# Strassen sums kept in PSUM, a second product in another order, and a planner that knows an exclusion

## The chip, the cores and the metric

The kernel runs on one core of a Trainium2 chip. The metric is device time in microseconds, the median of several runs; the profile shows one execution, with its span from the first instruction to the last. Five engines take part: TensorE (PE in the rows, its weight loads PEld), VectorE (DVE), ScalarE (ACT), GpSimd (POOL) and SyncE (SP), which issues most of the DMAs.

## The reference

Three parts follow each other, in float32, for a batch of 8 with 576 tokens and width 512:

1. Linear attention with 8 heads: `phi(x) = [exp(p), exp(-p)]` with `p = x @ w_phi - max|x @ w_phi|`, then `num / den` from `phi(k)^T v` and the sum of `phi(k)`.
2. A gated mixer: `(sigmoid(conv5(x)) * (x @ w_val)) @ w_out`, with a causal convolution of 5 taps per channel.
3. An FFT mixer and an MLP: `u = x + Re(fft2(x))`; `un` is the layer norm of `u`; the output is `u + relu(un @ w_ch1) @ w_ch2`, with 2048 hidden units.

This change lies in the third part, in the MLP and in the last FFT steps that are planned together with its start.

## The kernel before

Every product in float32 is made of float32r pieces: an operand is split into a rounded part `h` (made by ScalarE) and a rest `l = x - h` (a subtraction, on VectorE or GpSimd), and a product is three matmuls (`h*h`, `h*l`, `l*h`). A "split" below means both steps.

The MLP takes the tokens in 9 blocks of 512 (`NBK`) and the hidden units in 8 slices of 256 (`NJ`). Half of the weights is in SBUF at a time, so there are two passes over the blocks: the first with slices 0 to 3, blocks upwards, the second with slices 4 to 7, blocks downwards. A block of a pass is two units (`c` = 0, 1) of two slices each. The first pass computes the layer norm of each next block (`ln_stages`) and stores it; the second pass loads it again. Both passes make the seven split operands `un` of a block (`prep_un`) from tile `A`, of which there is one.

Both products of a unit use Winograd's form of Strassen's scheme: 7 products of 12 matmuls of 128x256 each instead of 8.

- `c1_units` makes the first product. Its seven products go to PSUM tiles `x` (two, used in turn by the units), `y` and `z`. ScalarE copies partial results to SBUF tiles `c11`, `c22` and `c12`; VectorE adds the later products to them; relu is on ScalarE; three subtractions of these SBUF tiles make the sums that Strassen's second product needs (noted after product 2), and each of the seven operands is split (`plain`, L813) into one of seven `h` slots.
- `c2_units` makes the second product from the `h` slots, in the order `SEQ2`, in PSUM tiles `cx`, `cy`, `cz`; `EVAC` says which tile a product goes to and to which of four SBUF accumulators `acc` VectorE then adds it.

The units are woven: the seven second products of one unit are noted between the seven first products of the next. Nothing is run in the order noted. `op` records an operation with what it reads and writes and with its cost for each engine that may do it: "v" VectorE, "a" ScalarE, "p" GpSimd, "m" TensorE, "d" DMA; "vp" leaves the choice between VectorE and GpSimd open. `place_ops` then plans: from the end backwards it gives each operation a due time, so that TensorE's work could run on without a gap; then, forwards, it takes again and again the operation that can start first on some engine, and among those ready on one engine the one due first. GpSimd gets an open operation only if it finishes it by the time VectorE would have, or by the due time. The engines' instruction order is the plan's order. `place_ops` runs twice: in `run_last` (the last two batches' FFT steps, the first block's layer norm and operands, the first weights) and in `run_mlp` (all the rest). Engine times (`free`) carry over from the first to the second.

The costs of the planner are a constant plus a slope per column, in microseconds (a matmul of the MLP has 0.109):

```
COST = {"v": (0.069, 1.042), "a": (0.09, 0.84), "p": (0.149, 2.1)}
```

Most of VectorE's and GpSimd's subtractions are recorded at the helpers' lines: L72 and L75 are the rests of a split on VectorE and on GpSimd, L648 any addition or subtraction, L651 a ScalarE copy or relu, L66 the rounded part of a split. L807 is the first product, L876 the second, L722 and L723 the means of the layer norm, L752 its reciprocal.

Of the kernel before, what the change touches and what calls it, by code (L numbers as in the profile page):

```python
# [23 lines left out]
TB = 512  # L24
# [5 lines left out]
def f32(ap):  # L30
    return ap.bitcast(F32)
# [3 lines left out]
def attention_moe_mixer_kernel(  # L35
# [540 lines left out]
    K = dict(hlo="vp", ht="vp", un="vp", ln="vp", w="vp", lat=0.2, lnat=6, bw=0.0028, dl=1.5, sq="a", su="a", ca=1, wl=1, win=0.0, marg=0.0, un0="vp", ln0="vp", w0="vp", t_lo="p", uf="vp")  # L576
# [7 lines left out]
    hs = []  # L584
# [47 lines left out]
    COST = {"v": (0.069, 1.042), "a": (0.09, 0.84), "p": (0.149, 2.1)}  # L632

    def op(e, cols, fn, reads, writes, dur=None, more=0.0):
        if dur is None:
            dur = {k: COST[k][0] + COST[k][1] * cols / 1000 for k in e}
        else:
            dur = {e: dur}
        ops.append((dur, fn, reads, writes, more))
# [4 lines left out]
    def o_lo(e, dst, src, hi, cols, r, w):  # L644
        op(e, cols, lambda e: (lo_dve if e == "v" else lo_pool)(dst, src, hi), r, w)

    def o_tt(e, o, x, y, alu, cols, r, w):
        op(e, cols, lambda e: (nc.vector if e == "v" else nc.gpsimd).tensor_tensor(out=o, in0=x, in1=y, op=alu), r, w)  # L648
# [143 lines left out]
    def c1_units(key, js):  # L792
# [5 lines left out]
        def product(i, n, first):  # L798
# [10 lines left out]
            op("m", 0, f, wk + [("un", i, 0), ("un", i, 1)] + ([] if first else [n]), [n, ("c1", key, i)], 12 * 0.109)  # L809
# [7 lines left out]
        def sub(o, p, r, e, rk, wk):  # L817
            o_tt(e, o, p, r, ALU.subtract, TB, rk, wk)

# [27 lines left out]
        s = sl[1] = h_free.pop(0)  # L847
        h, l = hs[s]
        o_act(h, x, ACTF.Relu, TB, [X], [("h", s, 0)])
        stt = nc.vector.scalar_tensor_tensor  # L850
        op("v", TB, lambda e: stt(out=l, in0=x, scalar=0.0, in1=f32(h), op0=ALU.max, op1=ALU.subtract), [X, ("h", s, 0)], [("h", s, 1)])
        plain(4, c11, "c11")
        plain(5, c22, "c22")
        plain(6, c12, "c12")
        op("v", TB, lambda e: stt(out=c22, in0=x, scalar=0.0, in1=c22, op0=ALU.max, op1=ALU.subtract), [X, "c22"], ["c22"])
        plain(3, c22, "c22")

    EVAC = {0: ("x", 0), 1: ("z", 0), 4: ("y", 3), 5: ("x", 1), 6: ("x", 3), 2: ("y", 1), 3: ("x", 2)}
    SEQ2 = (0, 1, 4, 5, 2, 6, 3)

    def c2_units(ps, t, c, key, js):
        for i in SEQ2:
# [15 lines left out]
            op("m", 0, f, wk + [("h", s, 0), ("h", s, 1)] + ([] if first else [ct]), [ct], 12 * 0.109)  # L878
# [23 lines left out]
    def note_W(b, ge, t, f, ps):  # L902
        gh, gl = ge
        for c in (0, 2, 1, 3):
            for a in range(2):
                k, p = next(ps)

                def prod(e, c=c, a=a, p=p):
                    for kk in range(4):
                        ws = slice(c * 128, (c + 1) * 128)  # L910
                        mm3(p[:, 0:NE], (wo[0][:, kk, ws], wo[1][:, kk, ws]), (gh[:, kk, a], gl[:, kk, a]), kk == 0, kk == 3)
                op("m", 0, prod, [], [k], 12 * 0.123)
                o_act(t[:, c, a, :], p[:, 0:NE], ACTF.Copy, NE, [k], [("x2", b, c, a)])
# [14 lines left out]
    def note_FD(b, f, y, ps):  # L928
# [4 lines left out]
        for j in range(3):  # L933
            n = 128 if j < 2 else 33
            sl = slice(128 * j, 128 * j + n)
            for a in range(2):
# [8 lines left out]
                op("m", 0, prod, fk + [("xr", 0), ("xr", 1)], [k], (7 - a) * 0.11)  # L945
# [18 lines left out]
    def note_SD(b, t, y, ps):  # L964
        yh, yl = y
        eo, u = tl["eo"], tl["u"]
        if b % 4 == 3:
# [3 lines left out]
               [("c256", e, i) for e in (b - 1, b) for i in range(5)], [k], 8 * 0.123)  # L971
# [6 lines left out]
        for i in range(2):  # L978
            ls = slice(128 * i, 128 * i + 128)
            for a in range(2):  # L980
# [6 lines left out]
                op("m", 0, prod, yk, [k], (8 - a) * 0.123)  # L987
# [82 lines left out]
    free = dict.fromkeys("mvapd", 0.0)  # L1070

    def place_ops():
# [3 lines left out]
        for i, (d, f, r, w, more) in enumerate(ops):  # L1076
# [19 lines left out]
        now = sum(o[0].get("m", 0) for o in ops)  # L1096
# [20 lines left out]
        end = [0.0] * n  # L1117
        for _ in range(n):
            best = None
            for e, q in ready.items():  # L1120
                cand = []
                for i in q:
                    d = ops[i][0]
                    if e == "p" and "v" in d:
                        t = max(free["p"], at[i])
# [14 lines left out]
            free[e] = t0 + ops[i][0][e]  # L1140
            start[i], end[i] = t0, free[e] + ops[i][4]
# [228 lines left out]
```

## Time and profile before

| | before |
|---|---|
| median of 3 runs | 1427.9 us (1426.38 to 1427.92) |
| profiled execution, span | 1426.1 us |
| TensorE busy, matmuls | 1346.5 us (94%) |
| VectorE busy | 1254.0 us (88%) |
| ScalarE busy | 814.0 us (57%) |
| GpSimd busy | 706.9 us (50%) |
| mean granted TensorE clock | 0.987 |

For the profiled execution the record has its span alone, and no total time of its own; the nearest run is 0.3 us above the span, the median 1.8 us. The attention takes about the first 320 us, the mixer and the FFT run to about 640, the MLP from there to the end. A VectorE record overlaps the next by about 0.08 us, so what an operation costs in a row of others is read from the distance of their starts.

### The profile page before, as it was taken

To read this page: it belongs to the slowest core of one execution; us is meant where nothing else is said; L and a number is where in the kernel's file an instruction comes from. 1 tells how busy PE (TensorE), PEld (TensorE's weight loads), DVE (VectorE), ACT (ScalarE), POOL (GpSimd) and SP (SyncE) were. 2 spreads that over 40 slices of the span, in tenths; PEclk is the share of its full clock that TensorE was granted. 3 is DMA by queue.
4 is the path that set the end of the run, shared out by engine and by line. 5 is a ranking of instruction groups with operands and counts; after the bars stand their busy time and mean duration, and the time that the engine had idled before them with its cause. 6 is when DMAs were issued, how large, how long until landed. Compare 5 with 4: busy or idle time off the path is not lost.

```text
span 1426.1 us, 35034 instructions
## 1 busy us (share of the span) xinstructions
PE 1346.5 (94%) x14672; PEld 1296.2 (91%) x14672; DVE 1254.0 (88%) x1938; ACT 814.0 (57%) x1513; POOL 706.9 (50%) x526
## 2 busy tenths in 40 slices
PE   8999989988999999967899899999999999999998
PEld 7888878877999999967799899999999999999998
DVE  6999999886999999798999999999899888778876
ACT  6888878763555545555455555555465455444442
POOL 3977888613576776464565455555335111111111
PEclk9999999998999999988999999999999999999999
DMA  7478867531344432335422232222433222122211
GB/s 257 149 259 301 275 240 254 207 148 52 104 141 141 141 139 103 120 129 181 134 93 93 90 119 92 94 82 89 141 109 104 82 81 84 60 90 90 89 42 48
DMA packets 89851, 186.98 MB, mean 131 GB/s; under 512 B 10455, under 2 KB 37335, under 8 KB 87518
## 3 DMA queue, kind: packets, MB, share of 16 engines
q1 hardware_dynamic: 88488, 181.33, 37.3%
q10 hardware_dynamic: 1206, 3.41, 0.6%
q8 instruction: 115, 1.88, 0.5%
q14 instruction: 42, 0.34, 0.1%
HBM read 121.79 MB, written 62.93 MB: 130 GB/s over the span
## 4 chain that ended last, share of the span: by engine, by line
PE 48%; DVE 34%; issue 6%; ACT 4%; POOL 4%; DMA 3%; SPq 0%; DVEq 0%; POOLq 0%; ACTq 0%
PE cx L876 9%; PE x L807 9%; PE cy L876 5%; PE y L807 4%; PE kv L244 4%; DVE acc L425 4%; PE pj L205 3%; DVE A L648 3%; DVE c L648 3%; PE nm L283 3%; PE z L807 3%; DVE acc L648 2%; PE cz L876 2%; DVE y L215 2%; DVE s L752 2%
## 5 line engine op out<-in xcount | busy, mean ns | idle before, releaser
L876 PE MATMUL cx<-h,w 128*128 128x256 f32 x1152 | 176.4, 286 | 4.8 <-ACT h L66 2.5
L876 PEld LDWEIGHTS cx<-h,w 128*128 128x128 f32 x1152 | 158.4, 194 | 6.8 <-ACT h L66 3.1
L66 ACT ACTIVATE h<-c 128x512 fp32r<-128x512 f32 x180 | 111.6, 627 | 38.9 <-DVE c L648 22.4
L648 POOL TENSOR_TENSOR c<-c,c 128x512 f32<-128x512 f32 x35 | 49.8, 1422 | 165.0 <-ACT h L651 125.4
L648 DVE TENSOR_TENSOR acc<-cx,acc 128x512 f32<-128x512 f32 x144 | 97.9, 680 | 33.0 <-PE cx L876 32.3
L651 ACT ACTIVATE c<-c 128x512 f32<-128x512 f32 x108 | 67.9, 630 | 100.4 <-DVE c L648 99.1
L807 PE MATMUL x<-un,w 128*128 128x256 f32 x864 | 117.0, 285 | 7.6 <-DVE eo L648 6.9
L75 POOL TENSOR_TENSOR h<-c,h 128x512 fp32r<-128x512 f32 x33 | 48.3, 1466 | 149.2 <-ACT h L66 148.9
L876 PE MATMUL cy<-h,w 128*128 128x256 f32 x864 | 117.3, 284 | 4.6 <-DVE h L72 1.9
L807 PEld LDWEIGHTS x<-un,w 128*128 128x128 f32 x864 | 109.9, 193 | 8.2 <-issue 7.1
L425 DVE SCALAR_TENSOR_TENSOR acc<-xf,cw,acc 128x576 f32<-128x576 f32 x128 | 104.9, 819 | 12.1 <-ACT acc L423 11.2
L876 PEld LDWEIGHTS cy<-h,w 128*128 128x128 f32 x864 | 108.9, 191 | 7.0 <-DVE h L72 2.5
L72 DVE TENSOR_TENSOR h<-c,h 128x512 fp32r<-128x512 f32 x111 | 103.7, 935 | 1.2 <-ACT h L66 0.5
L212 DVE TENSOR_REDUCE m<-pj 128x8 f32<-128x1024 f32 (+1 forms) x80 | 88.5, 1107 | 9.7 <-PE pj L205 9.7
L244 PE MATMUL kv<-vraw,ke 128*64 128x66 f32 x2560 | 95.6, 228 | 0.5 <-DVE kvT L257 0.2
L205 PE MATMUL pj<-wp,kqraw 64*128 64x128 f32 x1152 | 89.2, 293 | 6.2 <-DMA kqraw<-in_k_dram 4.4
L244 PEld LDWEIGHTS kv<-vraw,ke 128*64 128x64 f32 x2560 | 83.4, 139 | 11.5 <-ACT ke L224 1.0
L205 PEld LDWEIGHTS pj<-wp,kqraw 64*128 64x128 f32 x1152 | 73.5, 193 | 20.0 <-issue 20.0
L283 PE MATMUL nm<-kvT,qe 128*64 128x65 f32 x2304 | 84.3, 225 | 7.3 <-issue 4.1
L215 DVE TENSOR_TENSOR y<-pj,m 128x1024 f32<-128x1024 f32 (+1 forms) x80 | 88.6, 1107 | 0.4
L75 POOL TENSOR_TENSOR ge<-gs,ge 128x580 fp32r<-128x580 f32 x32 | 46.8, 1461 | 78.7 <-ACT ge L66 78.7
L283 PEld LDWEIGHTS nm<-kvT,qe 128*64 128x64 f32 x2304 | 76.5, 140 | 9.6 <-issue 7.7
(249 smaller groups left out, 4218.3 us busy)
## 6 DMA issues: line engine op xcount, KB each, us to landing
raw<-in_w_ch_dram SPq DMA_DIRECT2D x16, 1024.0 KB, 6.0
wr<-w_scr SPq DMA_DIRECT2D x32, 448.0 KB, 3.6
vraw<-in_v_dram SPq DMA_DIRECT2D x16, 660.0 KB, 9.3
x_scr<-xT SPq DMA_DIRECT2D x32, 288.0 KB, 4.0
xf<-x_scr SPq DMA_DIRECT2D x8, 1152.0 KB, 5.7
out_dram<-acc SPq DMA_DIRECT2D x36, 256.0 KB, 2.2
kqraw<-in_k_dram SPq DMA_DIRECT2D x15, 576.0 KB, 5.5
kqraw<-in_q_dram SPq DMA_DIRECT2D x15, 576.0 KB, 7.4
```

Source lines behind the costliest of these rows:

```text
L66: nc.scalar.activation(out=dst, in_=src, func=ACTF.Copy)
L72: nc.vector.tensor_tensor(out=dst, in0=src, in1=f32(hi), op=ALU.subtract)
L75: nc.gpsimd.tensor_tensor(out=dst, in0=src, in1=f32(hi), op=ALU.subtract)
L205: mm(p[:, h, o:o + F], t[r, w, 128 * c:128 * c + 128], wp[r, :], start=True, stop=True)
L212: nc.vector.tensor_reduce(out=m, in_=pv, axis=AX.X, op=ALU.max, apply_absolute_value=True)
L215: nc.vector.tensor_tensor(out=y, in0=pv, in1=m.unsqueeze(3).to_broadcast([128, 2, 2 * n, F]), op=ALU.subtract)
L244: mm(t[p, w, :], e[:, a, h, j, p], tv[:, h, slot, :], start=slot % 5 == 0 and w == 0, stop=slot % 5 == 4 and w == 3, skip_group_check=True)
L283: mm(t[p, 2 * j + h, 0:65], e[:, a, h, j, p], kt[:, 2 * h + a, b, :], start=(a == 0), stop=(a == 1))
L425: nc.vector.scalar_tensor_tensor(out=acc, in0=shifted(t), scalar=cw[:, m, t:t + 1], in1=acc, op0=ALU.mult, op1=ALU.add)
L648: op(e, cols, lambda e: (nc.vector if e == "v" else nc.gpsimd).tensor_tensor(out=o, in0=x, in1=y, op=alu), r, w)
L807: mm(p[:, n], l, v[:, kt], start=first and n + kt + m == 0, stop=kt == 1 and m == 2, skip_group_check=True)
L876: mm(p[:, o], v, r[:, n], start=first and o + n + m == 0, stop=n + m == 3, skip_group_check=True)
```

## The change

Four things are changed at once.

1. In `c1_units` the sums go back into PSUM: VectorE writes `z + c11`, `y + c12` and the differences into `z`, `y` and `x` themselves, ScalarE's clamp of `y` writes `y`, and the splits read these PSUM tiles (`split` in place of `plain`). The splits and differences that read PSUM are VectorE's; only product 2's operand may still go to GpSimd (`h2`). The splits of operands 4, 5 and 6 are noted after product 2 instead of after product 3.
2. `SEQ2` is another order.
3. `op` marks operations with two SBUF inputs (`two`), and `place_ops` books GpSimd's operations and VectorE's marked ones on a common resource `x`, so that the plan never runs one of either at the same time.
4. Costs: GpSimd's `(0.149, 2.1)` becomes `(0.15, 2.25)`, a matmul 0.12 instead of 0.109 (0.134 instead of 0.123 in the FFT steps). Due times count from TensorE's booked time (`free["m"]`), and GpSimd's limit is moved by `behind`, TensorE's lag against its due times.

```diff
-    K = dict(hlo="vp", ht="vp", un="vp", ...
+    K = dict(h2="vp", un="vp", ...
...
-    COST = {"v": (0.069, 1.042), "a": (0.09, 0.84), "p": (0.149, 2.1)}
-
-    def op(e, cols, fn, reads, writes, dur=None, more=0.0):
+    COST = {"v": (0.069, 1.042), "a": (0.09, 0.84), "p": (0.15, 2.25)}
+
+    BANKS = {"x0", "x1", "y", "z", "cx", "cy", "cz", "mean", "ps"}
+
+    def op(e, cols, fn, reads, writes, dur=None, more=0.0, two=False):
+
+        two = two and not any(k in BANKS or k[0] in BANKS for k in reads)
...
+        ops.append((dur, fn, reads, writes, more, two))
...
-        def plain(i, v, n, e=K["hlo"]):
+        def sub(o, p, r, rk, wk):
+            o_tt("v", o, p, r, ALU.subtract, TB, rk, wk)
+
+        def clamp(o, x, rk, wk):
+            o_act(o, x, ACTF.Relu, TB, rk, wk)
+
+        def split(i, p, k, relu, e="v"):
             s = sl[i] = h_free.pop(0)
             h, l = hs[s]
-            o_hi(h, v, TB, [n], [("h", s, 0)])
-            o_lo(e, l, v, h, TB, [n, ("h", s, 0)], [("h", s, 1)])
...
+            if relu:
+                clamp(h, p, [k], [("h", s, 0)])
+                op("v", TB, lambda e: stt(out=l, in0=p, scalar=0.0, in1=f32(h), op0=ALU.max, op1=ALU.subtract),
+                   [k, ("h", s, 0)], [("h", s, 1)])
+            else:
+                o_hi(h, p, TB, [k], [("h", s, 0)])
+                o_lo(e, l, p, h, TB, [k, ("h", s, 0)], [("h", s, 1)])
...
         product(1, "z", True)
-        o_tt("v", c11, z, c11, ALU.add, TB, ["z", "c11"], ["c11"])
-        o_act(c11, c11, ACTF.Relu, TB, ["c11"], ["c11"])
-        plain(0, c11, "c11")
+        o_tt("v", z, z, c11, ALU.add, TB, ["z", "c11"], ["z"])
+        split(0, z, "z", True)
+        clamp(c11, z, ["z"], ["c11"])
...
-        o_act(c22, c22, ACTF.Relu, TB, ["c22"], ["c22"])
-        plain(2, c22, "c22")
+        clamp(c22, c22, ["c22"], ["c22"])
+        split(2, c22, "c22", False, K["h2"])
         yield
         product(2, "y", False)
-        o_tt("v", c12, y, c12, ALU.add, TB, ["y", "c12"], ["c12"])
-        o_act(c12, c12, ACTF.Relu, TB, ["c12"], ["c12"])
-        sub(c11, c12, c11, K["ht"], ["c11", "c12"], ["c11"])
-        sub(c12, c22, c12, K["ht"], ["c22", "c12"], ["c12"])
-        sub(c22, c22, c11, K["ht"], ["c22", "c11"], ["c22"])
+        o_tt("v", y, y, c12, ALU.add, TB, ["y", "c12"], ["y"])
+        clamp(y, y, ["y"], ["y"])
+        sub(z, y, c11, ["y", "c11"], ["z"])
+        sub(y, c22, y, ["c22", "y"], ["y"])
+        split(4, z, "z", False)
+        sub(z, c22, z, ["c22", "z"], ["z"])
+        split(5, z, "z", False)
+        o_act(c22, z, ACTF.Copy, TB, ["z"], ["c22"])
+        split(6, y, "y", False)
         yield
         product(3, X, False)
...
-        plain(4, c11, "c11")
-        plain(5, c22, "c22")
-        plain(6, c12, "c12")
-        op("v", TB, lambda e: stt(out=c22, in0=x, scalar=0.0, in1=c22, op0=ALU.max, op1=ALU.subtract), [X, "c22"], ["c22"])
-        plain(3, c22, "c22")
+        split(1, x, X, True)
+        op("v", TB, lambda e: stt(out=x, in0=x, scalar=0.0, in1=c22, op0=ALU.max, op1=ALU.subtract), [X, "c22"], [X])
+        split(3, x, X, False)
...
-    SEQ2 = (0, 1, 4, 5, 2, 6, 3)
+    SEQ2 = (0, 4, 5, 1, 6, 2, 3)
...
-        now = sum(o[0].get("m", 0) for o in ops)
+        now = free["m"] + sum(o[0].get("m", 0) for o in ops)
...
+        def first(i, e):
+            t = max(free[e], at[i])
+            return max(t, free["x"]) if e == "p" or e == "v" and ops[i][5] else t
+
+        behind = 0.0
...
-                        if t + d["p"] > max(max(free["v"], at[i]) + ahead + d["v"], due[i] + d["v"] - K["marg"]):
+                        if t + d["p"] > max(max(free["v"], at[i]) + ahead + d["v"], due[i] + behind + d["v"] - K["marg"]):
                             continue
...
             free[e] = t0 + ops[i][0][e]
+            if e == "p" or e == "v" and ops[i][5]:
+                free["x"] = free[e]
+            if e == "m":
+                behind = t0 - due[i]
```

## Rows read from the trace of the kernel before

**Rows 1.** Windows by stage: window, length, then busy us (instructions) of each engine, clock.

```profile
606.00:642.00 36.00, 24.81 (x155) 22.51 (x153) 35.67 (x52) 19.45 (x41) 22.74 (x13) 0.89 0.36 131
...
642.90:713.00 70.10, 57.36 (x416) 55.38 (x417) 63.25 (x84) 36.90 (x61) 33.09 (x23) 0.92 0.48 155
713.00:1034.00 321.00, 305.94 (x2487) 300.04 (x2486) 307.41 (x438) 170.43 (x308) 175.02 (x131) 0.99 0.30 99
...
1105.00:1390.00 285.00, 285.00 (x2389) 285.00 (x2388) 228.94 (x334) 139.38 (x234) 43.86 (x34) 1.00 0.24 77
```

**Rows 2.** VectorE's groups by form, 713 to 1034 us: busy, mean ns, idle before.

```profile
L72 DVE TENSOR_TENSOR h<-c,h 128x512 fp32r<-128x512 f32 x42 | 37.9, 905 | 0.6 <-ACT h L66 0.5
L648 DVE TENSOR_TENSOR A<-A,s 128x512 f32<-128x512 f32 x28 | 28.1, 1048 | 0.0
L648 DVE TENSOR_TENSOR c<-c,c 128x512 f32<-128x512 f32 x29 | 27.9, 961 | 0.0
L752 DVE RECIPROCAL s<-s 128x128 f32<-128x128 f32 x28 | 26.0, 932 | 0.0
...
L72 DVE TENSOR_TENSOR un<-T,un 128x512 fp32r<-128x512 f32 x16 | 17.3, 1083 | 0.2 <-ACT un L66 0.2
```

**Rows 3.** Timeline of VectorE in one first-pass block: start, duration.

```profile
912.09 0.68 DVE L648 TENSOR_TENSOR acc<-cx,acc 128x512 f32<-128x512 f32 x1
912.68 0.68 DVE L72 TENSOR_TENSOR un<-T,un 128x512 fp32r<-128x512 f32 x1
913.28 0.68 DVE L72 TENSOR_TENSOR h<-c,h 128x512 fp32r<-128x512 f32 x1
...
915.69 0.67 DVE L648 TENSOR_TENSOR acc<-cx,acc 128x512 f32<-128x512 f32 x1
...
917.46 1.78 DVE L648 TENSOR_TENSOR c<-c,c 128x512 f32<-128x512 f32 x1
919.16 0.68 DVE L648 TENSOR_TENSOR T<-A,T 128x512 f32<-128x512 f32 x1
...
928.15 0.42 DVE L648 TENSOR_TENSOR s<-A 128x256 f32<-128x256 f32 x1
```

**Rows 4.** Timeline of GpSimd in the same block.

```profile
915.68 1.30 POOL L75 TENSOR_TENSOR h<-c,h 128x512 fp32r<-128x512 f32 x1
916.94 1.75 POOL L75 TENSOR_TENSOR un<-T,un 128x512 fp32r<-128x512 f32 x1
...
925.53 0.74 POOL L648 TENSOR_TENSOR s<-A 128x256 f32<-128x256 f32 x1 [2.23 <-DMA A<-u_scr]
```

**Rows 5.** The chain that ended last: start, us, what.

```profile
905.54 2.86 DVE A L648 x4
...
949.64 2.87 DVE A L648 x4
```

**Rows 6.** The convolution's accumulation in PSUM: duration min/median/max in ns.

```profile
L425 DVE SCALAR_TENSOR_TENSOR acc<-xf,cw,acc x128: 799/814/1497, 301.8 to 580.2; 128x576 f32<-128x576 f32 x128
```

**Rows 7.** TensorE's waits, 642 to 713 us: us in total, times, longest.

```profile
PE x L807 <- DVE eo L648: 6.9, 1, 6.9
```

**Rows 8.** Timeline of VectorE before the MLP.

```profile
633.12 4.41 DVE L72 TENSOR_TENSOR un<-T,un 128x512 fp32r<-128x512 f32 x2
```

**Rows 9.** Timeline of all engines at the end of the second pass.

```profile
1385.32 1.60 PE L807 MATMUL y<-un,w 128*128 128x256 f32 x12
...
1386.96 0.69 DVE L648 TENSOR_TENSOR c<-y,c 128x512 f32<-128x512 f32 x1
...
1387.68 0.63 ACT L651 ACTIVATE c<-c 128x512 f32<-128x512 f32 x1 [1.56 <-DVE c L648]
...
1393.93 0.87 PE L807 MATMUL y<-un,wg 128*128 128x256 f32 x6
...
1409.66 1.60 PE L876 MATMUL cx<-h,w 128*128 128x256 f32 x12
...
1420.43 1.67 PE L876 MATMUL cx<-wg,w 128*128 128x256 f32 x12 [0.88 <-DVE acc L648]
```

More of the change, by code (lines that the diff above doesn't have):

```diff
@@ L638, in op @@
             dur = {e: dur}
-        ops.append((dur, fn, reads, writes, more))
+        ops.append((dur, fn, reads, writes, more, two))
     def o_hi(dst, src, cols, r, w):
@@ L644, in o_lo @@
     def o_lo(e, dst, src, hi, cols, r, w):
-        op(e, cols, lambda e: (lo_dve if e == "v" else lo_pool)(dst, src, hi), r, w)
+        op(e, cols, lambda e: (lo_dve if e == "v" else lo_pool)(dst, src, hi), r, w, two=True)
     def o_tt(e, o, x, y, alu, cols, r, w):
-        op(e, cols, lambda e: (nc.vector if e == "v" else nc.gpsimd).tensor_tensor(out=o, in0=x, in1=y, op=alu), r, w)
+        op(e, cols, lambda e: (nc.vector if e == "v" else nc.gpsimd).tensor_tensor(out=o, in0=x, in1=y, op=alu), r, w, two=True)
     def o_act(o, x, func, cols, r, w, **kw):
@@ L808, in product @@
             wk = [("w", 0, j % NJP, o, k) for j in js for o in range(2) for k in range(2)]
[L809 to L811 removed]
+            op("m", 0, f, wk + [("un", i, 0), ("un", i, 1)] + ([] if first else [n]), [n, ("c1", key, i)], 12 * 0.12)
+        def sub(o, p, r, rk, wk):
[3 more added lines that the diff above has]
+        def split(i, p, k, relu, e="v"):
             s = sl[i] = h_free.pop(0)
             h, l = hs[s]
[L814 to L818 removed]
+            if relu:
[5 more added lines that the diff above has]
+                o_lo(e, l, p, h, TB, [k, ("h", s, 0)], [("h", s, 1)])
+        stt = nc.vector.scalar_tensor_tensor
         product(0, X, True)
@@ L877, in c2_units @@
             wk = [("w", 1, j % NJP, o, k) for j in js for o in range(2) for k in range(2)]
-            op("m", 0, f, wk + [("h", s, 0), ("h", s, 1)] + ([] if first else [ct]), [ct], 12 * 0.109)
+            op("m", 0, f, wk + [("h", s, 0), ("h", s, 1)] + ([] if first else [ct]), [ct], 12 * 0.12)
             h_free.append(s)
@@ L970, in note_SD @@
             op("m", 0, lambda e, p=p: seq_pass(p[0:97, 0:NE], lambda j: (c[:, 2 * j, 0:97], c[:, 2 * j + 1, 0:97]), c[:, 4, 0:97], 0),
-               [("c256", e, i) for e in (b - 1, b) for i in range(5)], [k], 8 * 0.123)
+               [("c256", e, i) for e in (b - 1, b) for i in range(5)], [k], 8 * 0.134)
             rk = [("r256", e) for e in (b - 1, b)]
@@ L986, in note_SD @@
                 yk = [("Y", j, a, h) for j in range(2) for h in range(2)] + [("rem", a, h) for h in range(3)]
[L987 removed]
+                op("m", 0, prod, yk, [k], (8 - a) * 0.134)
                 if a == 0:
@@ L1069, in attention_moe_mixer_kernel @@
     key_at = {}
-    free = dict.fromkeys("mvapd", 0.0)
+    free = dict.fromkeys("mvapdx", 0.0)
     def place_ops():
@@ L1075, in place_ops @@
         pred = [set() for _ in range(n)]
-        for i, (d, f, r, w, more) in enumerate(ops):
+        for i, (d, f, r, w, more, two) in enumerate(ops):
             for k in r:
@@ L1123, in place_ops @@
                     d = ops[i][0]
+                    t = first(i, e)
                     if e == "p" and "v" in d:
-                        t = max(free["p"], at[i])
                         ahead = sum(ops[j][0]["v"] for j in ready["v"] if j != i and due[j] <= due[i] and at[j] <= t + 0.5)
-                        if t + d["p"] > max(max(free["v"], at[i]) + ahead + d["v"], due[i] + d["v"] - K["marg"]):
+                        if t + d["p"] > max(max(free["v"], at[i]) + ahead + d["v"], due[i] + behind + d["v"] - K["marg"]):
                             continue
-                    cand.append(i)
+                    cand.append((i, t))
                 if not cand:
                     continue
-                t0 = max(free[e], min(at[i] for i in cand))
-                i = min((i for i in cand if at[i] <= t0 + K["win"]), key=lambda i: (due[i], i))
-                t0 = max(t0, at[i])
+                t0 = min(t for i, t in cand)
+                i, t0 = min(((i, t) for i, t in cand if t <= t0 + K["win"]), key=lambda c: (due[c[0]], c[0]))
                 if best is None or t0 < best[0]:
```

11 lines of the change are left out of this document (3 added, 8 removed).

## The prediction

> **What bounds the kernel now.** I read the busy table by stage first [rows 1]. The MLP starts at 642.9 us. From 1105 to 1390 TensorE is busy for all of 285.00 us and makes 2389 matmuls, 0.1193 us each: that is its own pace, and nothing around it can make this stage shorter. Measured with it, the stage 642.9 to 713 holds 416 matmuls, 49.6 us of work in 70.1, so 20.5 us are lost; 713 to 1034 holds 2487, 296.7 us in 321, so 24.3 us are lost. The reader is to see beside it that VectorE is busy 307.41 of the 321 us there, against 228.94 of 285 later, and GpSimd 175.02 against 43.86. So the first pass over the tokens, which also has the layer norm and the operand splits to make, is where VectorE presses on TensorE; the second pass is TensorE's alone.
>
> Next is whether VectorE works or waits inside its instructions. The groups by form from 713 to 1034 [rows 2] are the four costliest forms whose two inputs both lie in SBUF. On a 128x512 tile such an operation can take 0.68 us (912.68 in [rows 3]); these took 0.905 (h), 1.048 (A by s), 0.961 (c minus c) and 1.083 us (un) on average. The excess is 42 x 0.225 + 28 x 0.368 + 29 x 0.281 + 16 x 0.403, or 34 us in 321, from these forms alone. The timeline shows what it is [rows 3, 4]: the subtraction at 917.46 lasts 1.78 us; GpSimd's operation that began at 916.94 ends at 918.69, and 0.55 us later VectorE's is through. It stood still until GpSimd had finished. The acc addition at 915.69 is no such case: it has one input in PSUM, and GpSimd's 1.30 us beside it is its undisturbed time. So far as these rows show, GpSimd and VectorE exclude each other only where VectorE has two SBUF inputs.
>
> The chain of waits gives the period: the layer norm's last multiplications begin at 905.54 and at 949.64 [rows 5], 44.1 us for one block of 512 tokens. Two units of 14 products of 12 matmuls and 8 matmuls for the means are 344 x 0.1193 = 41.0 us. The block loses 3.1 us, and holds at least 34 x 44.1/321 = 4.7 us in which VectorE stands still.
>
> **The change, part by part.**
>
> *Sums in PSUM.* In a unit (two hidden slices of a block) VectorE makes 14 operations on c11, c12, c22 and h. Before, 5 of them read PSUM and 9 (three subtractions, six splits) read SBUF twice and may go to GpSimd. After, 13 have a PSUM input and stay on VectorE; the split of product 2 alone is still open to both. Price of one: in [rows 3] the starts 912.09 (acc, a PSUM input), 912.68 (un, two SBUF inputs) and 913.28 lie 0.59 and 0.60 us apart. A PSUM input costs nothing more, undisturbed. The output now goes to PSUM in six of the 13, which no row of the MLP shows; the nearest is the convolution's in-place accumulation [rows 6], 0.814 us for 576 columns where 0.68 scales to 0.76. I take 0.60 to 0.65 a piece.
>
> A first-pass block then asks of VectorE: 26 such operations, 13.5 acc additions and 4 mean subtractions at 0.60, 26.1 us; 4 reciprocals at 0.93 a record [rows 2] less 0.06 of overlap, 3.5; 4 multiplications of A, 2.4: 32 us of 41, 33.3 at the dearer price (7.8 us of slack). Open to both engines are 2 splits, 11 operations of the operand preparation and 16 half-size ones of the layer norm; all on GpSimd (1.30 and 0.74 us [rows 4]) they are 13 x 1.30 + 16 x 0.74 = 28.7 us. With A's 2.4 us the shared time is 31 us. Everything fits in 41 us, where before 18 full-size operations more had to be shared. ScalarE gets one operation more, 14 instead of 13 a unit at about 0.6 us; it is busy 170 of 321 us [rows 1], so this is hidden.
>
> The Trainium skill says otherwise of the price: "Perfetto Trace Analysis", section "Optimizing Scalar/DVE Operations", gives a VectorE instruction some 60 ns of access overhead in SBUF and 125 ns in PSUM. By that, 16 operations of a block would each be 65 ns dearer, an estimated 1.0 us a block, which the slack still covers; the rows at 0.59 and 0.60 do not agree with it.
>
> *The planner.* It now books GpSimd and VectorE's two-SBUF operations as one resource, prices GpSimd's full-size operation at 1.30 us instead of 1.22, and a matmul at 0.12 instead of 0.109 us; the rows have 1.30 and 0.1193, so the plan comes nearer to what runs. Due times in the MLP's plan no longer start at zero but at TensorE's booked time, and are moved by what TensorE lags: before, all were too early, so GpSimd got an operation only if it would end it sooner; now it may use the whole slack. I price that from nothing (the slack is real) to 0.74 - 0.34 = 0.40 us for each half-size step of the layer norm (0.74 on GpSimd [rows 4]; 0.42 on VectorE [rows 3] less 0.08 of overlap).
>
> *Terms.* First pass, 713 to 1034: bounds 0 and 24.3 us. Since the standing still (4.7 us a block and more) exceeds the loss (3.1), and the list above fits with 8 us to spare, I take three quarters, 18 us: the plan stays a plan, and some exclusion is left. Start, 642.9 to 713: 20.5 us are lost, but the granted clock was 0.92 [rows 1], which alone is 0.08 x 70 = 5.6 us, and weights are still being loaded and split there, which nothing here touches; bounds 0 and half of it, 10, I take 5, between them. Stage before, 606 to 642: VectorE busy 35.67 of 36 us [rows 1], two operand splits lasting 4.41 us instead of 1.3 [rows 8]; TensorE's first MLP product waits 6.9 us for VectorE [rows 7], which is the most to be had; one GpSimd operation set worse costs 2; I take 3. Second pass: 0.
>
> *The other order of the second product.* It was (0,1,4,5,2,6,3), with results in banks x,z,y,x,y,x,x: at the very end two products for bank x follow each other, and the last waits 0.88 us for VectorE to empty it [rows 9]. The order (0,4,5,1,6,2,3) gives x,y,x,z,x,y,x. The last unit's seven start at 1409.66, would need 7 x 1.43 = 10.0 us, and the last is issued through at 1420.43 + 1.43 = 1421.9: 2.2 us are lost. Bounds 0 and 2.2, I take 1.5. Between units the order is hidden, since a product of the first kind stands between any two. The accumulators' stores and loads (4 each a block, on SP's queue) are issued in the order of the new sequence, as many as before, and nothing on TensorE waits for one of them in the second pass.
>
> Sum: 18 + 5 + 3 + 1.5 = 27.5 us, from a span of 1426.1 to 1398.6. The median of the runs lies 1.8 us above that span, so the forecast is 1400 us.
>
> **The rivals.**
>
> *The layer norm's loop stays.* Tile A is single: its last read is at 919.16 [rows 3], the next block's first addition at 925.53, after a load [rows 4], and the multiplications at 949.64 close the loop, 44.1 us. It must become 3.1 us shorter. For: if GpSimd takes ten of the sixteen half-size steps to use their slack, they are 10 x 0.40 = 4 us longer, which eats most of the 4.7 us gained. Against: VectorE's queue, in which these steps stood, is 10 us a block shorter. Then the first pass gives 4 us instead of 18, the start and the stage before 4: 1428 - 4 - 4 - 1.5, 1418 us.
>
> *All goes.* The upper bounds 24.3 + 10 + 6.9 + 2.2, 43 us: 1385. For: the slack of 8 us on VectorE. Against: the start depends on weight loads that nothing here touches.
>
> *The sums hold their banks (the other side).* y used to be free after one addition. Now it holds sums until product 6's splits are done, and the next unit's product 4 needs it. In [rows 9] a y product starts at 1385.32, VectorE reads y at 1386.96, and the next y product starts at 1393.93: 7.0 us. The new chain is addition 0.7, clamp on ScalarE 0.63, two subtractions 1.3, ScalarE's copy 0.63 and VectorE's split 0.7: 4.0 us, with 3.0 us left for at most five other VectorE operations, and product 5 or another second product can go first if y is late. If these run out, TensorE stands, and every later product behind product 4 in its queue with it; at one product (1.43 us) in each of 34 units this costs 49 us: 1400 + 49, 1449 us. It decides from 27.5/34, 0.8 us a unit. Were the Trainium skill's 65 ns ("Perfetto Trace Analysis", as above) true of all operations in that window, they would take an estimated 0.7 us of the 3.0.
>
> *No change.* What VectorE is spared comes back because GpSimd, given more slack, ends splits just when they are due; each one that slips by the length of a GpSimd operation costs a TensorE wait of 1.3 us, and two or three a block use up the 3.1 us: about 1427 us.
>
> **How the numbers follow.** Likeliest case 0.50, its own range 1389 to 1412; loop stays 0.15; all goes 0.13; banks held 0.12; no change 0.10. What a measurement of this kernel can tell from no change is about 0.2%, 3 us. Of "no change" 0.07 falls within it and 0.02 above; so faster 0.79, same 0.07, slower 0.14. The range is 1385 to 1428: what lies below is some 0.06, half of "all goes", above 0.14.
>
> **What would show it.** Right: the groups by form have h, c and z, y operations at about 0.68 us with no second, longer mean; the period of the layer norm's multiplications falls from 44.1 to 41 to 42 us; VectorE is busy some 80% of the first pass; the stage at TensorE's own pace stays at 0.1193 us a matmul. Wrong: gaps of TensorE ended by VectorE or ScalarE writing y or z in the second pass; a period still of 44 us with GpSimd on the half-size steps; or VectorE's operations with a PSUM output well above 0.65 us apart. The forecast fails most easily in the first pass, which carries 18 of the 27.5 us.

## The result and the profile after

The changed kernel takes 1400.95 us (median of 4 runs, 1397.87 to 1401.37) against 1427.14 us (1424.96 to 1427.92) for the kernel before, run beside it: a ratio of 0.9821, 95% interval 0.9804 to 0.9837. The forecast was 1400. The profiled execution took 1397.87 us, 2.5 us more than its span. Two lines of its page:

```profile
span 1395.4 us, 35053 instructions
...
PE 1331.4 (95%) x14672; PEld 1287.4 (92%) x14672; DVE 1201.1 (86%) x1992; ACT 817.2 (59%) x1549; POOL 604.7 (43%) x472
```

GpSimd does 102 us less than before, and VectorE does not do more for it: 53 us less. The windows by stage of the changed kernel follow, the first as in [rows 1], the others set from the MLP's start, which is now 10 us earlier (window, length, then busy us and instructions of TensorE, its weight loads, VectorE, ScalarE, GpSimd, then the granted clock); the last line is three blocks in the middle of the first pass:

```profile
606.00:642.00 36.00, 22.11 (x148) 20.47 (x146) 33.42 (x51) 16.40 (x33) 15.22 (x10) 0.91 0.41 146
632.90:703.00 70.10, 57.69 (x421) 55.58 (x422) 61.44 (x96) 37.76 (x64) 17.79 (x12) 0.89 0.54 182
703.00:990.00 287.00, 282.50 (x2354) 281.38 (x2353) 268.06 (x456) 164.82 (x310) 104.36 (x95) 1.00 0.29 96
1060.00:1360.00 300.00, 300.00 (x2515) 300.00 (x2514) 227.56 (x351) 146.37 (x259) 46.85 (x37) 1.00 0.25 79
811.37:936.47 125.10, 124.03 (x1034) 123.51 (x1033) 116.14 (x199) 71.98 (x136) 46.39 (x43) 1.00 0.31 102
```

The same three blocks of the kernel before, in the same view:

```profile
826.92:959.27 132.35, 126.92 (x1035) 124.14 (x1033) 128.06 (x184) 70.93 (x130) 71.92 (x58) 1.00 0.29 96
```

The reader is to see the third line of the changed kernel: 2354 matmuls in 287 us take 0.1219 us each, where [rows 1] have 321/2487 = 0.1291 and TensorE's own pace is 0.1193. From the last line of the changed kernel and the line of the kernel before, three blocks went from 132.35 to 125.10 us, 44.1 to 41.7 a block. The second pass was at TensorE's pace before and is now (300/2515 = 0.1193). The start hardly got faster: 421 matmuls in 70.1 us where 416 were. (Line numbers have moved: what was L648, L651 and L752 is now L652, L655 and L756; the first product is L811, the second L886.)

Stage by stage, with a block counted from its first product of the first kind (every 168th such matmul):

| stage | before | after | difference | foretold |
|---|---|---|---|---|
| before the MLP (last step of the FFT's operand at ScalarE to the first product) | 52.3 | 48.0 | -4.3 | -3 |
| first pass, blocks 1 and 2 | 92.9 | 96.4 | +3.6 | -5 |
| first pass, blocks 3 to 9 | 312.0 | 289.8 | -22.1 | -18 |
| second pass | 361.8 | 360.4 | -1.4 | 0 |
| from the last first product to the last second product | 12.3 | 11.6 | -0.7 | -1.5 |

(The windows of the prediction ended at 713 and 1034, a little off the limits of blocks.) The work is not quite the same stage by stage: blocks 1 and 2 hold 616 matmuls now and held 604, blocks 3 to 9 2402 and 2415. Less their matmuls at 0.1193 us each, blocks 1 and 2 lose 2 us more than before, and blocks 3 to 9 lose 3.3 us where they lost 23.9. The table's differences add up to a gain of 25.0 us; the medians differ by 26.2. The spans differ by 30.7, because the profiled execution also left the mixer 5.7 us earlier, in code that the change leaves alone. That point lies between 583.3 and 590.9 us over all the profiles here, so I compare stages from the MLP on, and whole times by medians.

VectorE's groups by form, 703 to 985 us (busy, mean ns, idle before), answer to [rows 2]:

```profile
L652 DVE TENSOR_TENSOR A<-A,s 128x512 f32<-128x512 f32 x28 | 18.3, 708 | 0.0
L72 DVE TENSOR_TENSOR h<-z,h 128x512 fp32r<-128x512 f32 x21 | 14.4, 685 | 0.0
L652 DVE TENSOR_TENSOR z<-y,c 128x512 f32<-128x512 f32 x14 | 9.7, 692 | 0.0
L652 DVE TENSOR_TENSOR z<-c,z 128x512 f32<-128x512 f32 x14 | 9.6, 688 | 0.0
L72 DVE TENSOR_TENSOR un<-T,un 128x512 fp32r<-128x512 f32 x7 | 4.8, 688 | 0.4
```

No form has a long mean any more. A by s has two SBUF inputs as it had, and fell from 1048 to 708 ns: what changed is not the operation but what GpSimd does beside it. I count as standing still what VectorE's operations without a PSUM input take over 0.68 us for 512 columns and over 0.42 us for 256 [rows 3]: that was 7.0 us in a middle block before, and is less than 0.1 now.

### The profile page after: what moved, and what is told of

It reads as the page before. It is cut to its first block, busy times and chain, and to the rows that moved or that the text cites. A ratio compares the mean times of both kernels' runs of the same rounds, so it can differ in the third digit from the quotient of the medians.

```text
span 1395.4 us, 35053 instructions
## 1 busy us (share of the span) xinstructions
PE 1331.4 (95%) x14672; PEld 1287.4 (92%) x14672; DVE 1201.1 (86%) x1992; ACT 817.2 (59%) x1549; POOL 604.7 (43%) x472
## 4 chain that ended last, share of the span: by engine, by line
PE 59%; DVE 27%; issue 4%; POOL 4%; ACT 3%; DMA 2%; SPq 0%; ACTq 0%; DVEq 0%; POOLq 0%
PE x L811 14%; PE cx L886 13%; PE cy L886 7%; PE y L811 6%; PE cz L886 4%; DVE y L215 3%; DVE acc L425 3%; PE z L811 3%; DVE m L212 3%; PE kv L244 3%; PE pj L205 2%; PE nm L283 2%; DVE cv L94 2%; DVE s L756 2%; DVE gs L456 2%
## 5 line engine op out<-in xcount | busy, mean ns | idle before, releaser
L886 PE MATMUL cx<-h,w 128*128 128x256 f32 x1260 | 173.5, 283 | 2.9 <-DVE acc L652 2.7
L886 PEld LDWEIGHTS cx<-h,w 128*128 128x128 f32 x1260 | 161.2, 191 | 4.0 <-DVE acc L652 3.3
L811 PE MATMUL x<-un,w 128*128 128x256 f32 x864 | 118.4, 287 | 16.2 <-DVE eo L652 7.4
L75 POOL TENSOR_TENSOR un<-A,un 128x512 fp32r<-128x512 f32 x40 | 52.8, 1330 | 174.6 <-ACT un L66 171.0
L652 DVE TENSOR_TENSOR acc<-cx,acc 128x512 f32<-128x512 f32 x144 | 99.0, 687 | 33.9 <-PE cx L886 33.0
L811 PEld LDWEIGHTS x<-un,w 128*128 128x128 f32 x864 | 111.0, 195 | 17.1 <-issue 7.6
L886 PE MATMUL cy<-h,w 128*128 128x256 f32 x792 | 116.0, 284 | 0.0
L886 PEld LDWEIGHTS cy<-h,w 128*128 128x128 f32 x792 | 106.1, 193 | 0.0
L75 POOL TENSOR_TENSOR un<-T,un 128x512 fp32r<-128x512 f32 x39 | 51.0, 1309 | 105.8 <-ACT un L66 105.8
L80 PE MATMUL val<-xh,wv 128*128 128x288 f32 x256 | 76.7, 301 | 5.5 <-POOL xh L75 5.5
L99 POOL TENSOR_SCALAR mt<-mt 128x1024 f32<-128x1024 f32 (+1 forms) x21 | 55.7, 2651 | 50.6 <-DVE mt L97 37.1
L79 PE MATMUL val<-xh,wv 128*128 128x288 f32 x256 | 76.2, 300 | 0.7 <-DVE gv L452 0.7
```

The source lines that it names most:

```text
L75: nc.gpsimd.tensor_tensor(out=dst, in0=src, in1=f32(hi), op=ALU.subtract)
L79: mm(o, ah, bh, start=first, stop=False)
L80: mm(o, ah, bl, start=False, stop=False)
L811: mm(p[:, n], l, v[:, kt], start=first and n + kt + m == 0, stop=kt == 1 and m == 2, skip_group_check=True)
L886: mm(p[:, o], v, r[:, n], start=first and o + n + m == 0, stop=n + m == 3, skip_group_check=True)
```

## The experiments

Two theories. A, the prediction's: the sums in PSUM free VectorE and end the standing still, and the planner's edits are worth about nothing. B: the planner's edits put VectorE's queue in an order that fits what runs, and the sums matter little. "Blocks" is the time of the three middle blocks, "first two" that of blocks 1 and 2, "stage before" as above; medians and profile of each. The ratios are against the kernel before, run beside each group (1424.22 us beside e1 to e4, 1425.34 beside e5 to e9, 1425.66 beside e10 to e13).

| run | median (range) | ratio [95%] | blocks | first two | stage before |
|---|---|---|---|---|---|
| before | 1427.14 | 1 | 132.35 | 92.9 | 52.3 |
| after | 1400.95 | 0.9821 [0.9804, 0.9837] | 125.10 | 96.4 | 48.0 |
| e1 sums only | 1406.99 (1406.17 to 1411.84) | 0.9885 [0.9865, 0.9904] | 128.60 | 90.7 | 52.2 |
| e2 planner only | 1397.77 (1392.42 to 1398.05) | 0.9804 [0.9784, 0.9824] | 124.33 | 91.1 | 47.8 |
| e3 old order | 1394.66 (1386.67 to 1397.68) | 0.9772 [0.9741, 0.9804] | 125.14 | 91.0 | 47.8 |
| e4 no exclusion | 1420.73 (1416.89 to 1423.67) | 0.9974 [0.9961, 0.9987] | 129.15 | 93.5 | 54.6 |
| e5 old due | 1397.89 (1392.72 to 1400.32) | 0.9792 [0.9761, 0.9823] | 125.10 | 92.4 | 47.9 |
| e6 old costs | 1421.80 (1416.95 to 1425.03) | 0.9968 [0.9953, 0.9983] | 133.74 | 94.0 | 53.2 |
| e7 open work on GpSimd | 1415.58 (1411.78 to 1420.68) | 0.9927 [0.9898, 0.9956] | 134.17 | 92.6 | 48.0 |
| e9 exclusion only | 1418.01 (1415.40 to 1418.57) | 0.9943 [0.9925, 0.9961] | 131.54 | 93.6 | 53.4 |
| e10 old matmul cost | 1422.79 (1420.07 to 1424.83) | 0.9982 [0.9970, 0.9994] | 133.38 | 97.3 | 51.2 |
| e11 old GpSimd cost | 1404.22 (1402.65 to 1408.54) | 0.9858 [0.9841, 0.9876] | 128.50 | 96.1 | 48.1 |
| e12 old order again | 1395.35 (1392.61 to 1398.78) | 0.9792 [0.9774, 0.9811] | 125.13 | 91.4 | 47.9 |
| e13 changed again | 1400.74 (1397.37 to 1405.53) | 0.9832 [0.9810, 0.9853] | 125.10 | 97.1 | 47.9 |

(e11's three blocks hold 13 matmuls more than the others', 1.6 us.)

**e1 and e2: the sums alone, the planner alone.** Both have the old order of the second product. e1 is the change with the planner, costs and due times of before, against the changed kernel:

```diff
-    COST = {"v": (0.069, 1.042), "a": (0.09, 0.84), "p": (0.15, 2.25)}
+    COST = {"v": (0.069, 1.042), "a": (0.09, 0.84), "p": (0.149, 2.1)}
...
-            op("m", 0, f, wk + [("un", i, 0), ("un", i, 1)] + ([] if first else [n]), [n, ("c1", key, i)], 12 * 0.12)
+            op("m", 0, f, wk + [("un", i, 0), ("un", i, 1)] + ([] if first else [n]), [n, ("c1", key, i)], 12 * 0.109)
...
-    SEQ2 = (0, 4, 5, 1, 6, 2, 3)
+    SEQ2 = (0, 1, 4, 5, 2, 6, 3)
...
-        now = free["m"] + sum(o[0].get("m", 0) for o in ops)
+        now = sum(o[0].get("m", 0) for o in ops)
...
-            if e == "p" or e == "v" and ops[i][5]:
-                free["x"] = free[e]
-            if e == "m":
-                behind = t0 - due[i]
```

(The other matmul costs go back in the same way.) e2 is the kernel before with the new planner, costs and due times; against the changed kernel it has the first product's sums of before, throughout, and the old order (cut to its first lines and the order):

```diff
-        o_tt("v", z, z, c11, ALU.add, TB, ["z", "c11"], ["z"])
-        split(0, z, "z", True)
+        o_tt("v", c11, z, c11, ALU.add, TB, ["z", "c11"], ["c11"])
+        o_act(c11, c11, ACTF.Relu, TB, ["c11"], ["c11"])
+        plain(0, c11, "c11")
...
-    SEQ2 = (0, 4, 5, 1, 6, 2, 3)
+    SEQ2 = (0, 1, 4, 5, 2, 6, 3)
```

> The PSUM sums alone, with the old planner (no exclusion, old costs and due times) and the old order of the second product. Theory (VectorE standing still behind GpSimd costs the first pass, and PSUM operands escape it): most of the gain is here, 1405 to 1412 us, the period of the layer norm's multiplications 41.7 to 42.5 us instead of 44.1, the h and z groups at 0.68 to 0.70 us. Rival (the planner's truer prices made the gain): 1420 to 1427 us and a period of 43.5 us or more.

> The new planner alone (exclusion, costs, due times), with the sums in SBUF and the old order as in the kernel before. Theory: VectorE's two-SBUF operations and GpSimd's still need the same resource for some 38 us a block, so the period falls little, 43 to 44 us, and the time is 1415 to 1425 us. Rival (the planner made the gain): 1402 to 1410 us.

The sums alone give 17.2 us (1424.22 to 1406.99), the planner alone 26.5 us (to 1397.77), as much as the whole change and more than either forecast for it. The window of the three blocks of e2, and two of VectorE's groups by form there, 710 to 1000 us:

```profile
804.96:929.29 124.33, 124.25 (x1034) 123.54 (x1033) 119.85 (x193) 70.08 (x131) 58.61 (x49) 1.00 0.31 102
```

```profile
L72 DVE TENSOR_TENSOR h<-c,h 128x512 fp32r<-128x512 f32 x53 | 51.8, 976 | 2.0 <-ACT h L66 2.0
L652 DVE TENSOR_TENSOR A<-A,s 128x512 f32<-128x512 f32 x28 | 17.4, 656 | 0.0
```

TensorE works for 124.25 of 124.33 us, while the h splits still read SBUF twice and are still long, 976 ns: VectorE stands still for 3.0 us a block and TensorE hardly feels it. So theory A falls in what it says of the planner; that the sums free VectorE and gain something by themselves stands, since e1 has 2.6 us of standing still left in a block instead of 7.0, and blocks of 42.9 us instead of 44.1. The two parts are not additive: the sums are worth 17 us under the old plan, and under the new one 0 to 3 (e2 against e3, run side by side, 1397.77 and 1394.66, intervals overlapping).

**e3: the old order of the second product.** The changed kernel with one line undone:

```diff
-    SEQ2 = (0, 4, 5, 1, 6, 2, 3)
+    SEQ2 = (0, 1, 4, 5, 2, 6, 3)
```

> The changed kernel with SEQ2 as before. Prediction's term: 1.5 us slower than the changed kernel by the tail alone, 1402 us. What the changed kernel's tail shows (two products for cx are still last, 0.88 us of wait): no difference beyond 1 us. Rival (the order is needed for the PSUM sums, since operand 1 is now split last): TensorE waits for operand 1 in each unit, 1410 us or more.

1394.66 us, below all three forecasts, so the new order gains nothing; e12 and e13 below measure its loss.

**e4, e9: the exclusion.** e4 takes its booking out of the changed kernel, as here; e9 is the kernel before with the exclusion alone (the marks, the common resource and these lines that book it).

```diff
-            if e == "p" or e == "v" and ops[i][5]:
-                free["x"] = free[e]
```

> The changed kernel without the exclusion in the plan (the common resource is never booked). Theory: the PSUM sums leave little to exclude; VectorE's two-SBUF operations of the layer norm meet GpSimd's again, some 1 us of standing still a block: 1402 to 1406 us, period 41.8 to 42.3. Rival (the booking is what removes the standing still): 1412 us or more, with A by s and T, un groups above 0.9 us.

> The kernel before with the exclusion in the plan alone: old costs, old due times, sums in SBUF, old order. New theory: most of the planner's gain is here, 1398 to 1408 us, blocks of 41.5 to 42.5 us, VectorE's stage before the MLP 4 us shorter. Rival (it needs the truer costs and due times): 1413 us or more.

Without it the changed kernel loses nearly everything: 1420.73, with A by s at 927 ns again (710 to 1000 us); 6.6 of these 20 us lie in the stage before the MLP. Alone it gives 7.3 us (1425.34 to 1418.01), and the blocks stay at 43.8 us although the standing still is halved, 7.0 to 3.3 us a block. So the changed kernel needs the exclusion, and by itself it is not enough.

**e5: the due times.**

```diff
-        now = free["m"] + sum(o[0].get("m", 0) for o in ops)
+        now = sum(o[0].get("m", 0) for o in ops)
...
-            if e == "m":
-                behind = t0 - due[i]
```

> The changed kernel with due times from zero again and without TensorE's lag; exclusion, costs, sums and order as changed. New theory (the exclusion in the plan carries most of the gain, since without it the changed kernel lost 20 us): no difference beyond 4 us, 1397 to 1404 us, blocks of 41.4 to 42 us. Rival (the new due rule is what lets GpSimd's operations be placed well): 1408 us or more and blocks of 43 us.

1397.89 us with blocks of the same 125.10: this edit carries nothing of the gain.

**e6, e10, e11: the costs.** e6 has both old costs, e10 the old matmul costs alone (0.109, 0.11 and 0.123 for 0.12, 0.12 and 0.134), e11 the old GpSimd cost alone. Of e6's diff, the lines of GpSimd and of a second product:

```diff
-    COST = {"v": (0.069, 1.042), "a": (0.09, 0.84), "p": (0.15, 2.25)}
+    COST = {"v": (0.069, 1.042), "a": (0.09, 0.84), "p": (0.149, 2.1)}
...
-            op("m", 0, f, wk + [("h", s, 0), ("h", s, 1)] + ([] if first else [ct]), [ct], 12 * 0.12)
+            op("m", 0, f, wk + [("h", s, 0), ("h", s, 1)] + ([] if first else [ct]), [ct], 12 * 0.109)
```

> The changed kernel with the old costs (GpSimd 0.149 + 2.1 per 1000 columns, a matmul 0.109); exclusion, due times, sums and order as changed. New theory (exclusion): within 4 us, 1397 to 1405 us. Rival (with a GpSimd operation booked 0.08 us too short, each one planned close behind another runs into VectorE's next, and TensorE is planned 9% too fast): 1408 us or more, VectorE's two-SBUF groups above 0.75 us.

> The changed kernel with the matmul's old costs alone (0.109, 0.11 and 0.123 us); GpSimd's new price stays. Theory A (TensorE planned 9% too fast makes VectorE's order wrong: additions to acc are put where the plan has them ready, and TensorE then waits for them): as with both old costs, blocks of 44 to 45 us, 1415 to 1424 us, TensorE waiting some 2 us a block for acc. Theory B (GpSimd booked 0.08 us too short is what breaks the exclusion): blocks of 41.7 us, 1395 to 1404 us.

> The changed kernel with GpSimd's old price alone (0.149 + 2.1 per 1000 columns); the matmul's new costs stay. Theory A: blocks of 41.5 to 42 us, 1395 to 1404 us, some standing still of VectorE, below 1.5 us a block. Theory B: blocks of 43.5 us or more, 1413 us or more.

The matmul's price in the plan, 0.109 instead of 0.12 us, is worth 22 us in the changed kernel (e10 1422.79 against e13 1400.74, run side by side), as much as all of the blocks' gain; GpSimd's price 3.5 us (e11 against e13), with intervals that overlap. And the loss of e10 is not VectorE's standing still, which is 1.1 us a block. The timeline of all engines of e10 shows what it is (start, duration, what, and in brackets the idle time before and who ended it):

```profile
905.13 1.60 PE L886 MATMUL cx<-h,w 128*128 128x256 f32 x12
...
905.20 0.94 DVE L756 RECIPROCAL s<-s 128x128 f32<-128x128 f32 x1
...
906.61 1.86 DVE L756 RECIPROCAL s<-s 128x128 f32<-128x128 f32 x2
...
908.38 0.63 DVE L652 TENSOR_TENSOR A<-A,s 128x512 f32<-128x512 f32 x1
908.93 0.94 DVE L756 RECIPROCAL s<-s 128x128 f32<-128x128 f32 x1
...
909.78 2.92 DVE L652 TENSOR_TENSOR A<-A,s 128x512 f32<-128x512 f32 x3
...
912.62 0.68 DVE L652 TENSOR_TENSOR acc<-cx,acc 128x512 f32<-128x512 f32 x1
...
913.36 1.69 PE L886 MATMUL cx<-wg,w 128*128 128x256 f32 x12 [2.09 <-DVE acc L652]
```

The cx product is done at about 906.7, but its acc addition stands in VectorE's queue behind the reciprocals and the multiplications of A, and starts at 912.62; the next cx product has its turn and waits 2.09 us. In the waits of TensorE over three blocks of e10 (us in total, times, longest) it is the largest row, once a block:

```profile
PE cx L886 <- DVE acc L652: 6.3, 3, 2.1
```

In the changed kernel the same place reads so, TensorE's product first, then VectorE's timeline, then TensorE's waits over three blocks:

```profile
887.02 1.60 PE L886 MATMUL cx<-h,w 128*128 128x256 f32 x12
```

```profile
884.88 0.94 DVE L756 RECIPROCAL s<-s 128x128 f32<-128x128 f32 x1
885.79 0.69 DVE L652 TENSOR_TENSOR acc<-cx,acc 128x512 f32<-128x512 f32 x1
886.40 1.75 DVE L756 RECIPROCAL s<-s 128x128 f32<-128x128 f32 x2
888.07 2.43 DVE L652 TENSOR_TENSOR A<-A,s 128x512 f32<-128x512 f32 x4
890.41 0.68 DVE L72 TENSOR_TENSOR wg<-x,wg 128x512 fp32r<-128x512 f32 x1
891.01 0.68 DVE L652 TENSOR_TENSOR acc<-cx,acc 128x512 f32<-128x512 f32 x1
```

```profile
PE cx L886 <- DVE acc L652: 1.1, 3, 0.4
```

This cx product is done at about 888.6, when the reciprocals are already through. Its addition too stands behind the multiplications of A, but starts at 891.01, 2.4 us behind its product instead of 5.9, and the next cx product waits 0.36 us. The addition at 885.79, between the reciprocals, belongs to the cx product before it; in e10 that one (903.66) runs ahead of all four reciprocals. Same operations, same engines, but the layer norm's operations run some 4 us later against TensorE's products in e10 (first reciprocal at 905.20 beside a product at 905.13, here 883.43 and 887.02). Why the low price leads the planner to that place (a TensorE that it thinks 9% faster makes the next block's layer norm look due sooner) is argued, not shown; and since only 0.109 and 0.12 were run, it is not shown either that the true price is what matters and not just another one.

**e7: all of the MLP's open preparation on GpSimd.** This is the assumption of the prediction's capacity count.

```diff
-    K = dict(h2="vp", un="vp", ln="vp", w="vp",
+    K = dict(h2="vp", un="p", ln="p", w="vp",
```

> The changed kernel with every open operation of the layer norm and of the operand preparation forced to GpSimd in the MLP (28.7 us of GpSimd a block by the prediction's sum, against some 16 now). If capacity decides, as the prediction argued, 31 us of shared time fit in 41: blocks of 41.5 to 42.5 us, 1399 to 1407 us. If the loop through tile A decides (the rival that the layer norm's loop stays), its half-size steps are 0.40 us longer each, ten of them on the loop: blocks of 44 to 46 us, 1420 to 1440 us.

The window of its three blocks, and TensorE's largest wait in them:

```profile
829.31:963.48 134.17, 125.55 (x1035) 124.94 (x1033) 103.54 (x155) 71.55 (x135) 80.11 (x82) 0.99 0.29 95
```

```profile
PE cx L886 <- DVE acc L652: 8.6, 3, 2.9
```

GpSimd has 26.7 us of work a block (the prediction said 28.7), VectorE is busy 77% of the time, neither is full, and a block takes 44.7 us. Capacity does not decide the period; one addition that comes 2.9 us late in each block accounts for most of the 3.6 us lost. In VectorE's queue it stands right behind the four multiplications of A (910.69 to 914.11), as in e10. The first pass as a whole takes 404.5 us, as before (404.9). 1415.58 us lies between the two forecasts: of the 9.8 us by which the kernel is faster than before, 4.3 lie in the stage ahead of the MLP and 2.1 in the second pass and behind it; the rest was not followed.

**e12 and e13: the order again.** e3 and the changed kernel, run side by side on one chip.

> The changed kernel with the old order of the second product, the same as in the earlier run, now beside the changed kernel on one chip. If its 6 us are real, 1391 to 1398 us, the first pass 382 us; if they were the chip or the attention's scatter, within 2 us of the changed kernel.

> The changed kernel itself, for the comparison with the old order on the same chip: 1397 to 1402 us, first pass 386 us.

1395.35 against 1400.74: the new order costs 5.4 us. The intervals of the ratios, [0.9774, 0.9811] and [0.9810, 0.9853], just meet, so this is at the limit of the noise; e3 against after had the same sign. The windows of the first two blocks, e12 and then e13:

```profile
638.80:730.20 91.40, 80.79 (x604) 78.26 (x605) 82.05 (x135) 52.25 (x92) 27.00 (x21) 0.93 0.47 161
```

```profile
635.20:732.30 97.10, 81.65 (x617) 79.36 (x618) 86.70 (x137) 53.04 (x94) 28.39 (x23) 0.92 0.44 152
```

They differ by 5.7 us at nearly the same granted clock. The second holds 13 matmuls more, 1.6 us of work, which its later blocks have less. Over the whole first pass the new order costs 4.2 us (382.7 and 386.9 us); the middle blocks are equal. TensorE's waits in the start of the changed kernel, 625 to 703 us:

```profile
PE x L811 <- DVE eo L652: 7.4, 1, 7.4
PE x L811 <- ACT c L655: 4.2, 3, 2.7
PE x L811 <- ACT un L66: 3.3, 1, 3.3
PE x L811 <- DVE un L72: 2.8, 1, 2.8
```

The waits of 3.3 and 2.8 us for the next operands are missing with the old order. But e5, with the new order and the old due times, does not have them and takes 92.4 us in the first two blocks: it is not the order in itself but the plan that comes out of both. What in it moves these operands stays open.

The best version is thus the changed kernel with the old order: 1395.35 us, ratio 0.9792 to before. By their intervals e2 (the planner alone, 0.9804) and e5 (0.9792) are level with it.

## Why the prediction was right, and where it was not

**What bounds the kernel: right.** Of the 25.0 us, all but 2.1 were gained ahead of and in the first pass; the second pass moved by 1.4 of 361 us.

**The price of the sums in PSUM: right.** On VectorE's timeline of the changed kernel three additions follow each other, the first and last with PSUM at both ends:

```profile
849.90 0.69 DVE L652 TENSOR_TENSOR z<-z,c 128x512 f32<-128x512 f32 x1
850.50 0.69 DVE L652 TENSOR_TENSOR c<-x,c 128x512 f32<-128x512 f32 x1
851.10 0.69 DVE L652 TENSOR_TENSOR y<-y,c 128x512 f32<-128x512 f32 x1
```

They start 0.60 us apart, the cheap end of 0.60 to 0.65. The Trainium skill's dearer access to PSUM ("Perfetto Trace Analysis", "Optimizing Scalar/DVE Operations") is not to be seen in these rows either.

**The standing still: right that it goes, wrong that its length gives the loss.** The prediction set the 4.7 us of a block in which VectorE stands still beside the 3.1 us that the block loses, and took the one for the cause of the other. In the kernel before there is something in it. TensorE's longest wait in each middle block, 1.0 us, is for the PSUM tile x, which VectorE has yet to read, and ahead of that read (the last VectorE row below) in VectorE's queue stand operations that take 2.4 us more than they do undisturbed (four of 4.18 us in all, one of 1.40). The rows are VectorE's timeline, TensorE's, and TensorE's waits over three blocks:

```profile
905.46 4.18 DVE L648 TENSOR_TENSOR A<-A,s 128x512 f32<-128x512 f32 x4
...
910.17 1.40 DVE L648 TENSOR_TENSOR T<-A 128x512 f32<-128x512 f32 x1
911.48 0.68 DVE L648 TENSOR_TENSOR c<-x,c 128x512 f32<-128x512 f32 x1
```

```profile
912.22 0.98 PE L807 MATMUL x<-un,wg 128*128 128x256 f32 x6 [1.03 <-DVE c L648]
```

```profile
PE x L807 <- DVE c L648: 3.1, 3, 1.0
```

But that is one third of the loss, and over the runs the two do not go together: the loss being three blocks less their matmuls at 0.1193 us, e10 has 1.1 us of standing still in a block and loses 3.4 us; e2 has 3.0 and loses 0.3. The Trainium skill has the exclusion as the rows do ("SBUF — State Buffer", "Who interferes with whom": a VectorE instruction with two SBUF inputs contends with a GpSimd instruction that reads SBUF); 1048 to 708 ns for A by s agrees.

**The term that failed: the planner at nothing, or a loss.** The prediction noted that the new prices, 1.30 and 0.12, come nearer to the rows' 1.30 and 0.1193, and then priced this at zero to a loss of 0.40 us for a half-size step, and gave the whole 18 us of the first pass to the sums. For the sums by themselves the size was about right: in e1 the first pass is 17.7 us shorter (404.9 to 387.2), 15.4 of it in blocks 3 to 9. But the planner's edits alone give 26.5 us over the whole kernel, and the sums on top of them 0 to 3. In the changed kernel two edits of the planner are needed: without the exclusion (e4) 20 us are lost, with the old matmul price (e10) 22. These prices hold beside the other edits only. e1, with none of the planner's edits, takes 1406.99 us, while e4, e6 and e10, which lack one or two of them, take 1421 to 1423. About 5 us of that may be the new order, which e1 does not have; the rest means that here a part of the new planner is worse than none of it, and why was not followed. The matmul's price alone on the kernel before was not run.

GpSimd did not get more work, as feared for its due times, but less: 43 instructions in three blocks where 58 were. Part of that is that fewer operations are open to it with the sums in PSUM; but e2, where as many are open as before, has 49. That is also why VectorE is busy 93% of the middle blocks (116.14 of 125.10) and not the foretold 80%.

That the number came out right is in part luck. The sums and the planner remove the same loss, and the bound on that loss (24.3 us) was read from the right window; but blocks 3 to 9 gained 4 us more than foretold and the start came out 8.6 us worse, and with the smaller ones these misses cancel but for 2.5 us.

**The start: wrong sign.** Foretold -5, measured +3.6 in the first two blocks (some +2 for the same number of matmuls); e3 and e12 show that the change without its new order gives about -1.5 to -1.9 there.

**The stage before: right in size, -4.3 for -3.** It came from the planner too: e2 has 47.8 with the old sums, while e1, e4, e9, e6 and e10 stay at 51 to 55. And it did not come from the wait that the prediction named as the most to be had: TensorE's first MLP product waits 7.4 us for VectorE now, against 6.9 in [rows 7].

**The order of the second product: wrong sign.** The tail gained 0.7 us of the 1.5. The bank argument held for the order as noted, but at the end the planner ran product 2 (cy) ahead of 6, so the last two, 6 and 3, are again both in cx, and the last one waits as long as in [rows 9]:

```profile
1389.71 1.66 PE L886 MATMUL cx<-wg,w 128*128 128x256 f32 x12 [0.88 <-DVE acc L652]
```

Against it stand the 4.2 us of the first pass.

**The rivals.** The sums that hold their banks: not seen; between 990 and 1360 us TensorE has one wait to show.

```profile
PE cy L886 <- DVE wo L72: 0.6, 1, 0.6
```

The layer norm's loop: with the changed kernel's plan it closes in 41.7 us, so it did not bind; in e7 blocks of 44.7 us came back, with the acc addition as what TensorE waits for; that addition stands behind the multiplications of A, but whether tile A's loop sets the period there stays open. All goes: the middle blocks still lose 0.6 us each ((125.10 - 1034 x 0.1193)/3), where the rival had none. No change: it is what e6 and e10 came near to, by another way than foretold.

## What to carry to other kernels

Where a program fixes the order of in-order queues from a table of costs, check the table against the trace before touching the operations: beside the other edits, a matmul priced 9% low cost 22 us here, while moving the sums to another memory gave 17 us under the old plan and 3 at most beside the new one. Free capacity on an engine and time in which it stands still do not measure the loss; look for the one late instruction that the bounding engine waits for in each period, and see what stands ahead of it in its queue. And test the parts of a change singly and together, since two remedies for one loss do not add up, and a third part may cost something under their cover.

## What was unexpected

- VectorE can stand still 3.0 us in a block of 41.4 and be busy 96% of it (119.85 of 124.33, e2) while TensorE loses only 0.3 us a block; at 77% (e7) TensorE loses 3.6.
- The exclusion lengthens both sides: in [rows 4] GpSimd's own operation took 1.75 us instead of 1.30, besides VectorE's 1.78 instead of 0.68 in [rows 3].
- The stages ahead of the change end up to 7.7 us apart from one execution to the next, which is over a quarter of the gain; single spans can't be compared here.
